# Half-block sums and key-value products as 128x64 TensorE tiles, two steps on GpSimd, and a new order of work, in a four-layer attention kernel

## The chip, the cores and the metric

The kernel runs on one core of one Trainium2 chip. The metric is the device time of one execution in microseconds. Two runs of the kernel before gave 414.84 and 413.82, median 414.33.

A core has five engines with a queue each: PE (TensorE, matrix products), ACT (ScalarE), DVE (VectorE), POOL (GpSimd) and SP (here it only starts transfers). Each runs its own instructions strictly in order. Between engines the kernel waits on semaphores.

## What is computed

```python
x = A_x                                  # [1, 2048, 512], bf16
x = x + A(layernorm(x))                  # linear attention, 32 heads of 16
x = x + B(layernorm(x))                  # sliding-window softmax attention
x = x + A(layernorm(x))
x = x + B(layernorm(x))

# A: q, k, v = split(x @ wqkv);  phi(t) = where(t > 0, t + 1, exp(t)) + 1e-6
kv  = einsum("bhsd,bhse->bhde", phi(k), v);  z = einsum("bhsd->bhd", phi(k))
num = einsum("bhqd,bhde->bhqe", phi(q), kv); den = einsum("bhqd,bhd->bhq", phi(q), z) + 1e-6
A   = (num / den) @ wo

# B: W = 256, softmax over the keys with 0 <= query - key < W
p = softmax(where(mask, q @ k.T * 16 ** -0.5, -1e9))
B = (p @ v) @ wo
```

In A every row needs the sums `kv` and `z` over all 2048 rows, so no row of a layer A can finish before the last row of the layer before it. A layer B needs only the 256 rows before.

## The kernel before, in words

**Tiles and stages.** The 2048 rows are 16 row blocks of 128. Prefixes of the operations name the stage: `1.` is layer 1's pass over keys and values, `2.` is layer 1's queries and output and layer 2 (`2.b.` projections, `2.a.` attention), `2k.` is layer 3's keys and values, and `3.` is layer 3's queries and output and layer 4. Layers 2 and 3 overlap block by block: while some blocks are still in the attention of layer 2, others already make keys of layer 3.

**Layer A.** `a_kv` makes phi(k) (`pk`) and v with a column of ones (`vA`), and `kv_mm` adds their product into PSUM. One weight tile of 128 columns holds 8 heads, so the 128x136 product contains all pairs of these 8 heads, of which only the 8 diagonal blocks of 16x17 are wanted. It takes 4 matmuls a row block. In pass 1 all blocks add into one pair of PSUM banks; in pass `2k.` groups of 4, 4, 4, 2, 1 and 1 blocks do, and `acc` adds each group into `kvacc` on DVE, two instructions a group. `sums` multiplies by the block-diagonal mask `bm8` into `kvz`. `a_q` makes phi(q) with an exponential (ACT, L884), a minimum (DVE, L885), a relu (ACT, L887) and an addition (DVE, L888). `a_out` multiplies with `kvz` (L947), divides (L956 to L959) and goes through the output projection.

**Layer B.** `b_qkv` projects and lays keys out per head; values go by a small transfer from POOL's queue (`vbd`, L990). `b_attn` handles one row block. Its window is cut into pieces of 64 keys: four inner pieces that all 128 query rows see (`pF`) and two outer ones that only 64 query rows each see (`pH`; blocks 0 and 1 have one outer piece). Scores run as 32-row tiles of the array, four heads side by side (L1016 for `pH`, L1065 for `pF`); ACT takes exponentials (L1044, L1086); DVE multiplies by triangular masks (L1052 for `pH`, L1104 for `pF`); then PE multiplies the weights with the values: the inner sums (L1134) and the half-block sums (L1122; L1170 for the last block, in `b_end`). A half-block sum has only 64 query rows. Before, it is a full 128-column weight tile all the same: `pH` has 192 columns a head, the middle 64 are kept at zero (filled once by `fill_pH`, L705), and the slice of 128 columns is [rows 0 to 63, zeros] for one outer piece and [zeros, rows 64 to 127] for the other.

**Order.** Nothing is scheduled on the device. `ORDER` is a table of operation numbers, written out; each engine runs its operations in that order, `'` marks the second of two possible engines (for copies out of PSUM: ACT or DVE), and the numbers behind `:` are PSUM banks and buffers. `_Sched` derives the waits from what each operation reads and writes.

**Tile shapes on PE.** An operation has a mode: `f` for full 128x128 weight tiles, `r` for the 32-row tiles of the scores. Where a projection stands ahead of a change of mode, its last 512 columns are issued as 448 and 64 (`cut` in `proj_tok`).

Of the kernel before, what the change touches and what calls it, by code (L numbers as in the profile page):

```python
# [7 lines left out]
dt = mybir.dt  # L8
# [310 lines left out]
def _act_cost(n):  # L319
    return 0.055 + 0.000833 * n  # L320
# [23 lines left out]
617:4.3 618 619:0 448:2 405 851:0.2.0 415 852 853 416 631 592 632 417:3 625:7.2.5 406 633:0 626 878:4.0.1 622:6.3 623 648 879 880 649 467:3.10.3 468 627' 854  # L344
620 624' 634:4 428:4.0 429 873 469 418:3 650 593 449:2 471 882:0.6.2 883 884 450 482:3.11.1 483 855:1 860:0 861 856 430 431 470 857 621 432:1 451 484 903
651:1 858:1 935:4.6.0 486 862 863:2 859:0 864 885 419:2 420 421 635:3.4 936 874:0.4.3 485 872 433:0 652:0 636 937 607:2.0.0 875 876 608 909:0.6.4 637':1 904
910 911 865:1 62 609' 640:3.0 641 666 653:2.5 638 913:0.4.5 628 654 914 915 643:7.1.1 644 877 886:6 639 667 881 642' 668 629 610 611 655':2 669:2 912 891:3
887 970:0.4.1 645 646 888 702 703 889:3 890:2 938 866:2 892 893 971 972 67 656 894:0 895 657 905:0.6.0 906 867 434:5 435 868 907 944:0.3.3 436 658:2.1 1391
945 908 946 458:6.1 659 459 684 460 472 661:5.2.2 662 670:1 461 660 685 1392 462:3 686 704 917:0.3.1 1393 663' 921:2 922 923 463:2 896:3 918 919 948:0.6.2
924:2 647 916 920 671:5.0 949 950 672 473:3.3 925:1 474 705:3 926:2 1394:0 1395:0 927 487 475 687:1 673:0 1005:0.6.2 1006 476 477:0 928 676:5.2 677 929:0 930  # L350
1007 940:0.3.0 941 464:2 465 897:7 951 942 678' 979:0.5.4 980 688:3 706:2 478:1 931:0 1008 939 466 898 674 1401:4.1 1402 899 981 943 947 952:0.2.5 953
# [78 lines left out]
"""  # L430
PHIA = ("1.k","2.q","3.q")
HMD = ("2.a.", "3.a.")
BYPE = {("x1.", t) for t in range(4)} | {("a2.", 15), ("k2.", 15), ("o3.", 0), ("x3.", 0), ("a3.", 15)} | {("o2.",0),("x2.",0)}
VMOVE = {"POOL": 1.03}
KNEAR = {("3.b.", 0)}
LATE = 1


class _Kernel:
# [496 lines left out]
    def bmask(self, hf):  # L936
        return self.bm8.h[:].unsqueeze(1).unsqueeze(3).to_broadcast([P, 2, 8, 17])
# [443 lines left out]
```

## Time and profile before

| | |
|---|---|
| median of the two runs | 414.33 us (413.82 to 414.84) |
| the profiled execution | 414.87 us |
| span of the profile (first to last instruction) | 413.6 us |
| instructions | 18932 |
| TensorE clock granted | 1.00 |
| transfers from POOL's queue (`vbd`) | 128, 2.3 us to landing |
| transposing transfers on SP's queue (`oT`) | 60, 2.6 us to landing |

Busy times of the engines, the chain of waits and the groups of instructions are shown in the prediction, where they are used. "Busy" of PE includes the time in which a matmul runs out through the array, so it can read 97% where the matmuls themselves are issued less densely; the distance from one matmul's start to the next's is the better price. A group's "idle before" is the time that its engine stood still just ahead of it, and the name behind the arrow is what ended that.

### The profile page before, as it was taken

The page shows a single profiled execution, that of the slowest core. Times are in us where ns is not written, and L with a number is a line of the kernel's source. Part 1 is how long each engine was busy: PE and PEld are TensorE (multiplying, and loading weights), DVE is VectorE, ACT ScalarE, POOL GpSimd, SP SyncE. Part 2 cuts the span into 40 slices and gives each one's busy share as a digit, 9 for nine tenths or more (in the row PEclk, how much of TensorE's full clock was granted, in tenths as well). Part 3 has the DMA queues.
Part 4 walks back from the last instruction along what each step waited for, and adds up shares of the span by engine and source line. Part 5 has one row for each costly group of instructions (what it writes and reads, how often), then busy time and mean ns, then how long its engine had stood idle before and what let it go on. Part 6 is the DMA issues. An engine that isn't in the chain of part 4 may idle for free.

```text
span 413.6 us, 18932 instructions
## 1 busy us (share of the span) xinstructions
PE 399.4 (97%) x8394; PEld 284.3 (69%) x8394; DVE 370.5 (90%) x979; ACT 376.6 (91%) x485; POOL 104.8 (25%) x204
## 2 busy tenths in 40 slices
PE   7999999999999999999999999999999999999998
PEld 2654877776676767777686678676767776867765
DVE  6996799999999999999998999999999999887873
ACT  5998769999999999999999467899999999999996
POOL 2420025162053121411313000260533232311300
DMA  8539224526243235222122102331375453261433
GB/s 259 145 84 217 43 61 80 101 60 99 46 55 57 48 51 69 50 35 61 42 49 55 41 2 40 70 75 32 80 81 76 68 107 34 55 93 30 58 54 92
DMA packets 76808, 29.48 MB, mean 71 GB/s; under 512 B 66352, under 2 KB 74672, under 8 KB 76720
## 3 DMA queue, kind: packets, MB, share of 16 engines
q1 hardware_dynamic: 71424, 22.63, 29.7%
q0 software_dynamic: 4096, 4.46, 6.1%
q8 instruction: 68, 1.11, 1.2%
q10 hardware_dynamic: 1200, 1.11, 0.9%
q14 instruction: 20, 0.16, 0.2%
HBM read 6.29 MB, written 2.10 MB: 20 GB/s over the span
## 4 chain that ended last, share of the span: by engine, by line
PE 50%; ACT 34%; DVE 11%; DMA 3%; issue 1%; SPq 0%; DVEq 0%
ACT pF L1086 24%; PE ps L863 21%; PE ps L875 10%; ACT pH L1044 7%; PE ps L1134 6%; PE ps L1065 5%; PE ps L1122 3%; DVE o L959 2%; DMA w_Av<-in_A_wqkv_dram 2%; PE ps L1016 1%; DVE stats L819 1%; DMA oT<-o 1%; PE ps L921 1%; PE ps L947 1%; DVE pk L890 1%
## 5 line engine op out<-in xcount | busy, mean ns | idle before, releaser
L1086 ACT ACTIVATE pF<-ps 128x1024 bf16<-128x1024 f32 x240 | 229.6, 1083 | 4.4 <-PE ps L1065 2.6
L822 POOL TENSOR_TENSOR rstd<-mv,const 128x1 f32<-128x1 f32 x64 | 37.6, 594 | 211.9 <-DVE mv L820 194.2
L990 POOL DMA_DIRECT2D vbd<-vt x128 | 67.3, 533 | 73.8 <-DVE vt L850 48.6
L1134 PE MATMUL ps<-vbd,pF 128*128 128x34 bf16 x1856 | 62.2, 178 | 1.9 <-issue 1.9
L1044 ACT ACTIVATE pH<-ps 128x1024 bf16<-128x1024 f32 (+1 forms) x64 | 60.3, 1014 | 2.6 <-PE ps L1016 2.3
L1134 PEld LDWEIGHTS ps<-vbd,pF 128*128 128x128 bf16 x1856 | 54.7, 96 | 8.4 <-issue 2.1
L1104 DVE TENSOR_TENSOR pF<-pF,const 128x512 bf16<-128x512 bf16 (+2 forms) x116 | 47.1, 413 | 5.6 <-ACT pF L1086 5.2
L1065 PE MATMUL ps<-qT,kbd 32*128 32x128 bf16 x1920 | 48.7, 217 | 1.9 <-ACT pF L1086 0.6
L884 ACT ACTIVATE E<-ps 128x512 bf16<-128x512 f32 x64 | 38.6, 622 | 10.4 <-PE ps L875 7.8
L819 DVE BATCH_NORM_STATS2 stats<-xres 128x6 f32<-128x512 bf16 x64 | 43.4, 684 | 1.9 <-DMA xres<-in_A_x_dram 1.6
L1052 DVE TENSOR_TENSOR pH<-pH,const 128x1024 bf16<-128x1024 bf16 (+1 forms) x64 | 41.1, 644 | 0.4 <-ACT pH L1044 0.4
L1065 PEld LDWEIGHTS ps<-qT,kbd 32*128 32x128 bf16 x1920 | 28.2, 92 | 17.7 <-ACT pF L1086 7.0
L875 PE MATMUL ps<-xT,w_Bk 128*128 128x128 bf16 x512 | 35.5, 219 | 0.7 <-ACT xT L850 0.3
L875 PE MATMUL ps<-xT,w_Bq 128*128 128x128 bf16 x512 | 35.6, 219 | 0.2 <-ACT pF L1086 0.2
L1122 PEld LDWEIGHTS ps<-vbd,pH 128*128 128x128 bf16 x928 | 29.2, 96 | 9.4 <-issue 3.1
L863 PE MATMUL ps<-w_Av,xTa 128*128 128x512 bf16 (+2 forms) x134 | 33.9, 369 | 1.4 <-DMA w_Av<-in_A_wqkv_dram 1.2
L875 PE MATMUL ps<-xTa,w_Aq 128*128 128x128 bf16 x512 | 34.8, 219 | 0.2 <-DVE pq L888 0.2
L863 PE MATMUL ps<-w_Bv,xT 128*128 128x512 bf16 (+2 forms) x144 | 34.2, 356 | 0.6 <-ACT pF L1086 0.3
L863 PE MATMUL ps<-w_Bo,oT 128*128 128x512 bf16 (+2 forms) x141 | 34.5, 354 | 0.3
L1122 PE MATMUL ps<-vbd,pH 128*128 128x34 bf16 x928 | 32.8, 178 | 1.3 <-DVE pF L1104 0.5
L863 PE MATMUL ps<-w_Ao,oT 128*128 128x512 bf16 (+2 forms) x145 | 33.7, 354 | 0.2
L863 PE MATMUL ps<-w_Ak,xTa 128*128 128x512 bf16 (+1 forms) x131 | 32.7, 374 | 0.6 <-ACT xTa L850 0.5
(98 smaller groups left out, 611.1 us busy)
## 6 DMA issues: line engine op xcount, KB each, us to landing
vbd<-vt POOLq DMA_DIRECT2D x128, 34.0 KB, 2.3
xres<-in_A_x_dram SPq DMA_DIRECT2D x16, 128.0 KB, 5.7
out_dram<-xres SPq DMA_DIRECT2D x15, 128.0 KB, 2.3
oT<-o SPq DMA_TRANSPOSE x60, 2.6
w_Ak<-in_A_wqkv_dram ACTq DMA_DIRECT2D x1, 512.0 KB, 5.5
w_Av<-in_A_wqkv_dram ACTq DMA_DIRECT2D x1, 512.0 KB, 7.6
w_Aq<-in_A_wqkv_dram SPq DMA_DIRECT2D x1, 512.0 KB, 6.6
w_Ao<-in_A_wo_dram SPq DMA_DIRECT2D x1, 512.0 KB, 5.8
```

The source lines that it names most:

```text
L819: s.op(n + ".st", {"DVE": 0.595}, lambda e, en: e.bn_stats(st0, x.h[:]), reads=[x], writes=[st])
L863: i = e.matmul(g.h[:, a:b], xT.h[:, kt, :], w.h[:, kt, a:b], start=(kt == 0), stop=(kt == 3), skip_group_check=True)
L875: i = e.matmul(g.h[:, f * P:(f + 1) * P], w.h[:, kt, f * P:(f + 1) * P], xT.h[:, kt, :], start=(f == 0 and kt == 0), stop=(kt == 3), skip_ ...
L884: s.op(n + ".e", {"ACT": _act_cost(512)}, lambda e, en: e.activation(E.h[:], g.h, ACT.Exp, bias=0.0), reads=[g], writes=[E])
L990: return [e.dma_start(vbd.h[64 * a:64 * a + 64, j, a], vt.h[64 * j:64 * j + 64, a]) for j in range(2)]
L1044: return e.activation(d, c, ACT.Exp, bias=0.0, scale=DH ** -0.5)
L1052: return e.tensor_tensor(v, v, tr, ALU.mult)
L1065: i = e.matmul(ss[r // 2].h[:, r % 2, k * P:k * P + P], kbds[fj[m] // 2].h[32 * r:32 * r + 32, f, fj[m] % 2, :], qT.h[32 * r:32 * r + 32, ...
L1086: s.op("e%d%d" % (u, g), {"ACT": _act_cost(1024)}, lambda e, en, S=ss[g], pb=pb, g=g: e.activation(pb.h[:, 2 * g:2 * g + 2, :], S.h, ACT.E ...
L1104: return e.tensor_tensor(v, v, tr, ALU.mult)
L1122: i = e.matmul(U.h[:, c:c + 34], pH.h[:, 4 * r + f, 64 * a:64 * a + P], vbds[j // 2].h[:, j % 2, :, 4 * f + r, :], start=first[0], stop=Tr ...
L1134: i = e.matmul(U.h[:, c:c + 34], pFs[at[f, m][0]].h[:, r, at[f, m][1] * P:at[f, m][1] * P + P], vbds[fj[m] // 2].h[:, fj[m] % 2, :, 4 * f ...
```

## The change

1. **Half-block sums as 128x64 tiles.** `pH` shrinks to 128 columns a head, without the zeros. The two outer pieces of a head become two matmuls with 64 weight columns each, at column positions 0 and 64 of the array (`tile_position=(0, 64 * a)`), writing PSUM partitions 0 to 63 and 64 to 127. This is a third mode, `c`. With two outer pieces the half sums open the accumulator, ahead of the inner ones; with one, they come behind. They no longer list the `pF` tiles among what they wait for.
2. **Key-value products as 128x64 tiles.** 8 matmuls of 64 weight columns and 68 moving columns a row block in place of 4 of 128 and 136. The result fits one PSUM bank; pass 1 issues them in four groups of four blocks; `acc` becomes one DVE instruction a group, and `sums` four DVE instructions of 136 columns in place of two of 272.
3. **Row block 15's queries in layer 3**: the exponential is taken on POOL as a power of e (`q.w`, `ALU.pow`); DVE makes min(q, 0) into `xm` and max(q, 0), and the closing addition also adds 1e-6. ACT's exponential and relu of that block go.
4. **Row block 9 in layer 4**: the two `pH` masks go from DVE to POOL.
5. A new `ORDER`; row block 3's first transposition goes from PE to a transfer; `fill_pH` goes.

```diff
-BYPE = {("x1.", t) for t in range(4)} | {("a2.", 15), ("k2.", 15), ("o3.", 0), ("x3.", 0), ("a3.", 15)} | {("o2.",0),("x2.",0)}
+BYPE = {("x1.", t) for t in range(3)} | {("a2.", 15), ("k2.", 15), ("o3.", 0), ("x3.", 0), ("a3.", 15)} | {("o2.",0),("x2.",0)}
-LATE = 1
+KV1 = [4, 4, 4, 4]
+KV2 = [4, 4, 4, 2, 1, 1]
+PHIP = set()
+POWQ = {("3.", 15)}
+MPOOL = {("3.a.", 9)}
...
-            self.r_pH = self.preset("pH", 3, [P, 16, 192], self.fill_pH())
+            self.r_pH = self.ring("pH", 3, [P, 16, P])
...
     def phi(self, n, g, E, o, view, t=None):
+        if n == "q" and (s.at[0], t) in POWQ:
+            xm, base = self.r_xm.buf(), self.base
+            s.op(n + ".n", {"DVE": _dve_cost(512)}, lambda e, en: e.tensor_scalar(xm.h[:], g.h, 0.0, None, op0=ALU.min), reads=[g], writes=[xm], new=[xm])
+            s.op(n + ".r", {"DVE": _dve_cost(512)}, lambda e, en: e.tensor_scalar(view(o), g.h, 0.0, None, op0=ALU.max), reads=[g], writes=[o])
+            s.op(n + ".w", {"POOL": 3.0}, lambda e, en: e.tensor_tensor(E.h[:], base.h[:].to_broadcast([P, D]), xm.h[:], ALU.pow), reads=[xm, base], writes=[E])
+            s.op(n + ".a", {"DVE": 0.335}, lambda e, en: e.scalar_tensor_tensor(view(o), E.h[:], 1e-6, view(o), op0=ALU.add, op1=ALU.add), reads=[E], writes=[o])
+            return
...
                 for f in range(4):
-                    i = e.matmul(d[f // 2][:, (f % 2) * 136:(f % 2) * 136 + 136], pk.h[:, f * P:(f + 1) * P],
-                                 vA.h[:, 8 * f:8 * f + 8, :], start=(start and n == 0 and f % 2 == 0), stop=True,
-                                 skip_group_check=True)
+                    for c in range(2):
+                        i = e.matmul(g.h[64 * c:64 * c + 64, f * 68:f * 68 + 68], pk.h[:, f * P + 64 * c:f * P + 64 * c + 64],
+                                     vA.h[:, 8 * f + 4 * c:8 * f + 4 * c + 4, :], start=(start and n == 0 and f == 0), stop=True,
+                                     skip_group_check=True, tile_position=(0, 64 * c))
...
-            s.op("mH%d" % g, {"DVE": 0.065 + 0.00054 * 512 * len(pcs)}, mkH, reads=[self.tri, mH[g]], part=[pH])
+            s.op("mH%d" % g, {"POOL": 1.5} if (s.at[0], t) in MPOOL else {"DVE": 0.065 + 0.00054 * 512 * len(pcs)}, mkH, reads=[self.tri, mH[g]], part=[pH])
...
                         for a, j in pcs:
                             c = ((f % 2) * 4 + r) * 34
-                            i = e.matmul(U.h[:, c:c + 34], pH.h[:, 4 * r + f, 64 * a:64 * a + P], vbds[j // 2].h[:, j % 2, :, 4 * f + r, :],
-                                         start=first[0], stop=True, skip_group_check=True)
-                            first[0] = False
+                            i = e.matmul(U.h[64 * a:64 * a + 64, c:c + 34], pH.h[:, 4 * r + f, 64 * a:64 * a + 64], vbds[j // 2].h[:, j % 2, :, 4 * f + r, :],
+                                         start=(len(pcs) == 2 and f == 2 * g and r == 0), stop=True, skip_group_check=True, tile_position=(0, 64 * a))
...
-            s.op("u%dh" % g, {"PE": 0.0255 * 8 * len(pcs)}, pvH, reads=[pH] + [vbds[j // 2] for _, j in pcs] + (pFs[2 * g:2 * g + 1 + LATE] if m0 == 0 else use(2 * g)),
-                 writes=[U], new=[U], kind="sum")
+                s.op("u%dh" % g, {"PE": 0.27 if side else 0.25}, pvH, reads=[pH] + [vbds[j // 2] for _, j in pcs], writes=[U], new=new, mode="c", kind="sum")
...
-                    for hf in range(2):
-                        d = self.kvacc[:, 2 * hf:2 * hf + 2, :].rearrange("p f c -> p (f c)")
-                        i = e.tensor_copy(d, g2[hf].h[:, 0:272]) if ngrp == 0 else e.tensor_tensor(d, g2[hf].h[:, 0:272], d, ALU.add)
-                    return i
+                    d = self.kvacc[:].rearrange("p f c -> p (f c)")
+                    return e.tensor_copy(d, g2.h[:, 0:272]) if ngrp == 0 else e.tensor_tensor(d, g2.h[:, 0:272], d, ALU.add)
```

How the order moves is shown at three places. The first is PE in the stretch where layer 2's attention and layer 3's keys and values interleave. Rows name line, operation, output and inputs, and the tile; `pH` rows are half-block sums, `pF` rows with `vbd` inner sums, `qT,kbd` scores. Before:

```order
L1065 MATMUL ps<-qT,kbd 128x128 x16
L1122 MATMUL ps<-vbd,pH 128x34 x16
L1134 MATMUL ps<-vbd,pF 128x34 x16
L1122 MATMUL ps<-vbd,pH 128x34 x16
L1134 MATMUL ps<-vbd,pF 128x34 x16
L1016 MATMUL ps<-qT,kbd 128x64 x32
L1134 MATMUL ps<-vbd,pF 128x34 x16
L875 MATMUL ps<-xT,w_Bq 128x128 x8
```

The same stretch after the change (lines have moved: L1064 is the inner scores, L1119 the half-block sums, L1135 the inner sums):

```order
L1064 MATMUL ps<-qT,kbd 128x128 x16
L860 MATMUL ps<-w_Bo,oT 128x512 x3
L860 MATMUL ps<-w_Bo,oT 128x448
L860 MATMUL ps<-w_Bo,oT 128x64
L1119 MATMUL ps<-vbd,pH 64x34 x16
L1064 MATMUL ps<-qT,kbd 128x128 x16
L1135 MATMUL ps<-vbd,pF 128x34 x16
L1119 MATMUL ps<-vbd,pH 64x34 x16
L1135 MATMUL ps<-vbd,pF 128x34 x16
L1016 MATMUL ps<-qT,kbd 128x64 x32
```

Before, half sums and inner sums follow each other in one tile shape; after, each group of half sums stands between others as a shape of its own (64x34). Counted along PE's whole order, the tile shape changes 306 times before and 380 times after, the projections cut into 448 and 64 columns are 59 and 82, and the matmuls of the half sums are 960 both times.

The second place is PE at the end of pass `2k.`, where the last key-value products of layer 3 are made and its queries' products (`kvz,pq`) begin. Before:

```order
L921 MATMUL ps<-vA,pk 128x136 x16
L863 MATMUL ps<-w_Ak,xTa 128x512 x4
L863 MATMUL ps<-w_Av,xTa 128x512 x4
L921 MATMUL ps<-vA,pk 128x136 x8
L863 MATMUL ps<-w_Av,xTa 128x512 x4
L921 MATMUL ps<-vA,pk 128x136 x4
L875 MATMUL ps<-xTa,w_Aq 128x128 x8
L921 MATMUL ps<-vA,pk 128x136 x4
L875 MATMUL ps<-xTa,w_Aq 128x128 x32
L947 MATMUL ps<-kvz,pq 128x136 x8
```

The same place after:

```order
L860 MATMUL ps<-w_Ak,xTa 128x512 x4
L860 MATMUL ps<-w_Av,xTa 128x512 x7
L860 MATMUL ps<-w_Av,xTa 128x448
L860 MATMUL ps<-w_Av,xTa 128x64
L925 MATMUL ps<-vA,pk 64x68 x64
L872 MATMUL ps<-xTa,w_Aq 128x128 x32
L947 MATMUL ps<-kvz,pq 128x136 x10
```

Before, the products of the last eight blocks stand in four groups with projections between them; after, they are one run of 64, with 32 matmuls of the query projection (`w_Aq`) between them and the first product with `kvz`. On DVE the four `kvacc` additions and the four `kvz` instructions that lie between these two stand directly behind each other.

The third place is DVE and POOL at the power of row block 15 in layer 3. DVE after the change, with buffer numbers; `xm` is the input of the power, `rstd` comes from POOL:

```order
L883 TENSOR_SCALAR xm_95<-ps 128x512
L902 TENSOR_TENSOR xres_23<-ps,xres_23 128x512 [waits s_PE]
L816 BN_STATS stats_1<-xres_23 128x6 [waits s_DVE]
L956 TENSOR_SCALAR dn_119<-ps 128x32 [waits s_PE]
L817 BN_AGGR mv_38<-stats_1 128x2 [waits s_DVE]
L958 RECIPROCAL dn_119<-dn_119 128x32 [waits s_DVE]
L959 TENSOR_TENSOR o_113<-ps,dn_119 128x512 [waits s_DVE]
L822 TENSOR_SCALAR xn_43<-xres_23,mv_38,rstd_39 128x512 [waits s_POOL]
```

And POOL:

```order
L819 TENSOR_TENSOR rstd<-mv,const 128x1
L885 TENSOR_TENSOR E<-const,xm 128x512
L819 TENSOR_TENSOR rstd<-mv,const 128x1
L990 DMA vbd<-vt 64x272 x4
```

On POOL the power stands ahead of the `rstd` that the last DVE row waits for. The result of the power itself is read 144 DVE rows after `xm` is written. Counted along ACT's order, copies out of PSUM on ACT change from 8 to 10 (`kt`), 12 to 9 (`qT`), 11 to 8 (`vt`) and 5 to 4 (`xTa`), and one small `oT` copy comes from DVE; on DVE they change from 23 to 21, 20 to 23 and 21 to 24.

More of the change, by code (lines that the diff above doesn't have):

```diff
@@ L1134, in pvF @@
                             i = e.matmul(U.h[:, c:c + 34], pFs[at[f, m][0]].h[:, r, at[f, m][1] * P:at[f, m][1] * P + P], vbds[fj[m] // 2].h[:, fj[m] % 2, :, 4 * f + r, :],
-                                         start=False, stop=True, skip_group_check=True)
+                                         start=(not side and f == 2 * g and r == 0 and m == m0), stop=True, skip_group_check=True)
                     return i
-                s.op("u%d%d" % (g, f % 2), {"PE": 0.0252 * 4 * (4 - m0)}, pvF, reads=use(f) + [vbds[j // 2] for j in fj[m0:]], writes=[U], kind="sum")
+                s.op("u%d%d" % (g, f % 2), {"PE": 0.0252 * 4 * (4 - m0)}, pvF, reads=use(f) + [vbds[j // 2] for j in fj[m0:]], writes=[U],
+                     new=[U] if not side and f == 2 * g else [], kind="sum")
+            if not side:
+                half([])
             dn = self.r_dn.buf()
@@ L1169, in pvH @@
                     for a, j in pcs:
-                        i = e.matmul(U.h[:, r * 34:r * 34 + 34], pH.h[:, 4 * r + f, 64 * a:64 * a + P], vbds[j // 2].h[:, j % 2, :, 4 * f + r, :],
-                                     start=(r == 0 and j == pcs[0][1]), stop=True, skip_group_check=True)
+                        i = e.matmul(U.h[64 * a:64 * a + 64, r * 34:r * 34 + 34], pH.h[:, 4 * r + f, 64 * a:64 * a + 64], vbds[j // 2].h[:, j % 2, :, 4 * f + r, :],
+                                     start=(r == 0), stop=True, skip_group_check=True, tile_position=(0, 64 * a))
                 return i
-            s.op("z%dh" % f, {"PE": 0.0255 * 4 * len(pcs)}, pvH, reads=[pH] + [vbds[j // 2] for _, j in pcs], writes=[U], new=[U], kind="sum")
+            s.op("z%dh" % f, {"PE": 0.145}, pvH, reads=[pH] + [vbds[j // 2] for _, j in pcs], writes=[U], new=[U], mode="c", kind="sum")
             for hf in range(2):
@@ L1306, in graph @@
         s.at = ("1.", base)
-        self.sums(lambda hf: kvS.h[:, hf, 0:272], kvz)
+        self.sums(lambda: kvS.h[:, 0:272], kvz)
         b1 = base + 0.1
@@ L1336, in graph @@
         s.at = ("2.", b2)
[L1337 removed]
+        self.sums(lambda: self.kvacc[:].rearrange("p f c -> p (f c)"), kvz2)
         self.segment("3.", b2, xTs2, kvz2, True)
```

217 lines of the change are left out of this document (110 added, 107 removed), and 70 rows, old and new, of the table ORDER.

## The prediction, made before the changed kernel had run

> **What bounds the kernel now.** I read the page's head first (span, busy time of each engine, shares of the chain that ended last), then the busy times by stage, then PE's timeline in the attention.
>
> ```profile
> span 413.6 us, 18932 instructions
> PE 399.4 (97%) x8394; PEld 284.3 (69%) x8394; DVE 370.5 (90%) x979; ACT 376.6 (91%) x485; POOL 104.8 (25%) x204
> PE 50%; ACT 34%; DVE 11%; DMA 3%; issue 1%; SPq 0%; DVEq 0%
> ```
>
> Three engines are at 90% or above, and the chain alternates between PE (half of the span) and ACT (a third). So no single engine can be made faster alone for full pay. By stage (stretch in us; then its length; then busy us and instructions of PE, weight loads, DVE, ACT, POOL; clock; DMA share; GB/s):
>
> ```profile
> 0.00:20.00 20.00, 17.10 (x120) 9.26 (x121) 16.25 (x56) 14.88 (x23) 6.45 (x23) 1.00 0.67 201
> 80.00:200.00 120.00, 117.51 (x2722) 84.87 (x2720) 112.37 (x286) 116.39 (x141) 35.74 (x66) 1.00 0.36 60
> 200.00:280.00 80.00, 77.89 (x1464) 57.15 (x1461) 74.75 (x200) 67.15 (x96) 17.56 (x32) 1.00 0.25 47
> 280.00:400.00 120.00, 116.99 (x3024) 85.02 (x3028) 108.21 (x267) 118.68 (x133) 32.99 (x62) 1.00 0.41 62
> ```
>
> In the two long attention stretches (240 us) PE is busy 234.5 us and ACT 235.1 us: both are full. Between 200 and 280, where the keys of layer 3 are made, ACT has 12.9 us to spare and PE 2.1 us. The clock is 1.00 throughout, so it plays no part.
>
> **Prices on PE.** Starts and busy time of PE's instructions in the attention of layer 4; a matmul's price is the distance from its start to the next start:
>
> ```profile
> 296.82 0.60 PE L863 MATMUL ps<-w_Bo,oT 128*128 128x512 bf16 x3
> 297.35 0.40 PE L1065 MATMUL ps<-qT,kbd 32*128 32x128 bf16 x16
> 297.68 0.61 PE L863 MATMUL ps<-w_Bo,oT 128*128 128x512 bf16 x2
> 298.13 0.56 PE L1122 MATMUL ps<-vbd,pH 128*128 128x34 bf16 x16
> 298.54 0.96 PE L1134 MATMUL ps<-vbd,pF 128*128 128x34 bf16 x32
> 299.43 0.40 PE L1065 MATMUL ps<-qT,kbd 32*128 32x128 bf16 x16
> 299.81 0.57 PE L1122 MATMUL ps<-vbd,pH 128*128 128x34 bf16 x16
> 300.23 1.03 PE L863 MATMUL ps<-w_Ao,oT 128*128 128x512 bf16 x5
> 301.19 0.41 PE L1016 MATMUL ps<-qT,kbd 32*128 32x64 bf16 x32
> 301.53 0.97 PE L1134 MATMUL ps<-vbd,pF 128*128 128x34 bf16 x32
> ...
> 311.35 0.40 PE L947 MATMUL ps<-kvz,pq 128*128 128x136 bf16 x4
> 311.58 0.60 PE L863 MATMUL ps<-w_Bo,oT 128*128 128x512 bf16 x3
> ```
>
> There is next to no gap between them: PE is issue-bound here. Half sums: 298.54 − 298.13 = 0.41 us for 16, so 25.6 ns each. The 128x136 product: 0.23 us for 4, 58 ns. A full 512-column product: 298.13 − 297.68 for two, 0.225 us.
>
> A change of tile shape: 32 inner sums at 25.6 ns would take 0.82 us but 0.89 pass to the scores at 299.43, so 0.07 us go on the way in. 16 scores of 128 columns, four side by side, stream as many columns as one 512-column product, 0.225 us; 0.33 pass (297.35 to 297.68), so 0.105 go on the way out; the 32 scores of 64 columns give 0.34 − 0.225 = 0.115. I take 0.088 us a change, the mean of 0.07 and 0.105, and keep 0.07 and 0.115 as ends. The same rows give what tiles side by side cost: 32 scores of 64 columns are 8 sets of four in 0.225 us, 28 ns a set.
>
> **The change on PE.**
>
> ```profile
> L1122 PE MATMUL ps<-vbd,pH 128*128 128x34 bf16 x928 | 32.8, 178 | 1.3 <-DVE pF L1104 0.5 <-ACT kt L850 0.2 <-ACT qT L850 0.2
> L1170 PE MATMUL ps<-vbd,pH 128*128 128x34 bf16 x32 | 1.4, 179 | 0.0
> L921 PE MATMUL ps<-vA,pk 128*128 128x136 bf16 x128 | 10.0, 223 | 0.1
> ```
>
> Half sums: 928 + 32 = 960. Blocks 0 and 1 of both layers B have one outer piece, 64 matmuls without a partner, whose price I leave. The other 896 become 448 pairs. Before, a pair costs 2 × 25.6 = 51.2 ns. No row shows two column tiles side by side. Below lies 25.6 ns (a pair for the price of one), above 51.2 (one after the other); the nearest row is the set of four row tiles, 28 ns, and I take 30. Gain 448 × 21.2 = 9.5 us, ends 0 and 11.5.
>
> Key-value products: 128 × 58 ns = 7.4 us become 128 pairs of 68 columns. From the same row, a little more for the wider tile, 32 ns: 4.1 us. Gain 3.3, ends 0.9 (51.2 a pair) and 3.8 (28).
>
> Changes of shape: 380 instead of 306, 74 × 0.088 = 6.5 us lost, ends 5.2 and 8.5. Net on PE 9.5 + 3.3 − 6.5 = **6.3 us less**, ends 10.1 less and 7.6 more. The 23 further cut projections issue the same columns; row block 3's four transposes that leave PE are four matmuls. I take both at nothing.
>
> **ACT and DVE.**
>
> ```profile
> L884 ACT ACTIVATE E<-ps 128x512 bf16<-128x512 f32 x64 | 38.6, 622 | 10.4 <-PE ps L875 7.8 <-PE ps L863 2.4
> L887 ACT ACTIVATE pq<-ps 128x512 bf16<-128x512 f32 x32 | 19.9, 634 | 2.9 <-PE ps L875 2.8
> L850 ACT ACTIVATE kt<-ps 128x512 bf16<-128x512 f32 x8 | 4.9, 616 | 1.7 <-PE ps L875 1.6
> L850 DVE CAST kt<-ps 128x512 bf16<-128x512 f32 x23 | 15.7, 681 | 0.3 <-PE ps L875 0.2
> L1328 DVE TENSOR_TENSOR kvacc<-ps,kvacc 128x272 f32<-128x272 f32 x10 | 3.9, 433 | 0.0
> L1232 DVE TENSOR_TENSOR kvz<-kvacc,const 128x272 bf16<-128x272 f32 x2 | 0.8, 438 | 0.0
> L1052 DVE TENSOR_TENSOR pH<-pH,const 128x1024 bf16<-128x1024 bf16 x56 | 37.8, 678 | 0.4 <-ACT pH L1044 0.4
> ```
>
> ACT loses block 15's exponential (0.62) and relu (0.63) and five copies net (+2 − 3 − 3 − 1, at 0.62: 3.1), and gains a small one I put at 0.3: **4.1 us less**. The filling of `pH` also goes, at the start, where ACT is busy only 14.9 of 20 us; I take it at nothing, since ACT waits there for the first projections.
>
> DVE gains four copies net (4 × 0.68 = 2.7) and loses six `kvacc` instructions (6 × 0.43 = 2.6). Four `kvz` instructions become eight of half the width: from the same time to twice 1.75 us, so 0 to 1.75 more. Block 15: two reads of 512 columns out of PSUM come (1.36), and one minimum goes. Two masks go (1.36). About 1 us more in 370, on an engine that has 11% of the chain: 0.1.
>
> At the end of pass `2k.` DVE makes four `kvacc` and four `kvz` instructions in a row, 4 × 0.43 + 4 × 0.22 to 0.44 = 2.6 to 3.5 us, while PE has 32 matmuls of the query projection in front of the first product that needs them. Before, two and two stood there (1.7 us) behind the same 32. PE will stand for what is not covered; with the products' own run of 32 pairs as further cover I put 0.5 us, ends 0 and 1.5.
>
> **POOL.**
>
> ```profile
> L822 POOL TENSOR_TENSOR rstd<-mv,const 128x1 f32<-128x1 f32 x64 | 37.6, 594 | 211.9 <-DVE mv L820 194.2 <-DVE dn L956 15.9 <-DVE const L724 1.7
> L731 POOL IOTA const<- 128x128 int32 x1 | 0.2, 227 | 0.0
> L735 POOL MEMSET const<- 128x1 f32 x1 | 0.1, 91 | 0.0
> L898 DVE TENSOR_TENSOR xres<-ps,xres 128x512 bf16<-128x512 f32 x32 | 21.7, 678 | 0.2 <-PE ps L863 0.2
> L819 DVE BATCH_NORM_STATS2 stats<-xres 128x6 f32<-128x512 bf16 x64 | 43.4, 684 | 1.9 <-DMA xres<-in_A_x_dram 1.6
> L958 DVE RECIPROCAL dn<-dn 128x32 f32<-128x32 f32 x32 | 10.9, 343 | 0.5
> L959 DVE TENSOR_TENSOR o<-ps,dn 128x512 bf16<-128x512 f32 x32 | 21.8, 684 | 0.5
> L1086 ACT ACTIVATE pF<-ps 128x1024 bf16<-128x1024 f32 x240 | 229.6, 1083 | 4.4 <-PE ps L1065 2.6 <-PE ps L1072 0.5
> ```
>
> The power over 512 columns has no row. `rstd` is the same operation on one column, 0.59 us, and an end from below; the index fill shows (227 − 91) / 127 = 1.1 ns a column for something much simpler, so 1.2 us is a better lower end, and 3 us my guess, from nothing better than between. Nobody needs its result soon (144 DVE instructions later). But the next `rstd` is queued behind it on POOL, and DVE waits for that one at `xn`. Between stand DVE's 0.68 + 0.68 + 0.34 + 0.68 = 2.4 us and two short ones; less the `rstd` itself, about 1.8 us cover the power. At 3 us DVE stands 1.2 us once, in a stretch where it is 93% busy. I count none of it in the time, since its later work is also fed late by PE, and keep 1.2 for the range; from there on every further us of the power is a us on DVE.
>
> The two masks (0.68 each on DVE) go ahead of four `vbd` transfers of a later block, and the first half sum of block 9 waits for POOL. In ACT's order six inner exponentials follow these two before the next half exponentials: four of them, some 4 us, lie ahead of the inner sum that PE issues right behind that half sum, so two masks of up to 2 us each are covered. None counted.
>
> The Trainium skill, page "SBUF — State Buffer", in the part on engine ports, says that DVE instructions with two SBUF inputs and GpSimd share one pair of ports as an exclusive lock for the whole instruction. By that rule these three POOL instructions would also hold up masks on DVE, and my sum would be up to their length, a few us, worse; no row here shows POOL with a long instruction.
>
> **The sum.** PE's part of the chain is 50% of 413.6, 207 us; PE's work shrinks by 6.3 of 399.4, which gives 3.3 us. ACT's part is 34%, 141 us; its work shrinks by 4.1 of 376.6, 1.5 us. Less 0.5 at pass `2k.` and 0.1 for DVE: 4.2 us. The profiled execution took 414.87 (span 413.6 and 1.3 around it), so 410.7; the median of the runs is 0.54 lower, so **410 us**, 1% faster. A measurement of this kernel tells about 2% (8.3 us) from no change, so this counts as "within 2%". With PE's and the stall's ends the forecast's own range is 405 to 414.
>
> **The rivals.**
>
> *The two column tiles don't run side by side.* Then the change doesn't do what it says: a pair still costs 51.2 ns, key-value products give 0.9 us, and 74 changes of shape cost 6.5: PE gets 5.6 us more work where it is issue-bound, and the time is **420 us, slower**. It decides from a pair price of some 41 ns on, where 448 × 10.2 + 128 × 17 ns = 6.7 us only just pays for the changes of shape; at 56 ns a pair it is slower by over 2%. For it: no row shows column tiles. Against: four row tiles in 28 ns show that the array takes several small tiles at once. The page "TensorEngine Tiling (Array Packing)" of the Trainium skill, in its restrictions, says that column tiling switches the fast weight load off, and "TensorE: Matmul & The Clock Gate", in its part on the weight load, gives the columns divided by 1.2 as the ns of a plain load: 53 ns for 64 columns, an estimate by which a pair would gain nothing even with both loads at once. No run here shows it yet. Chance 0.14.
>
> *PE's gain turns into waiting for ACT.* In 240 of 413 us ACT is as full as PE; if the shorter PE work only lets PE wait for exponentials there and ACT's 4.1 us come from stretches where it had time to spare, the time stays at **414**. For it: ACT is at 98% in those stretches. Against: ACT's copies that go lie there too. Chance 0.17.
>
> *All of it pays.* Pair at 26 to 28 ns, PE 10 us less, and the order moves exponentials into the 12.9 spare us between 200 and 280: **404**. Chance 0.12.
>
> *The power is long.* At 10 us on POOL, 8 us of waiting at `xn`, half of it recovered: **414 to 418**. Chance 0.06.
>
> **How the numbers follow.** Forecast 0.51. Faster by over 2% (under 406): most of the third rival (0.10) and the lower edge of the forecast (0.07), 0.17. Slower by over 2% (over 422.6): half of the first rival and a little of the last, 0.08. Within: 0.75. The range 404 to 419 leaves out 0.08 below and 0.11 above.
>
> **What would show it.** In the profile after, right: 16 half sums start to start in about 0.24 us plus a change; a change into or out of the narrow shape at 0.07 to 0.12; PE's rows still without gaps; ACT's busy time near 372. Wrong: half sums of 16 in 0.41 or more; `xn` on DVE waiting for `rstd` by more than a microsecond; PE standing behind exponentials by more in total than now; a gap in front of the first product with `kvz`.

## The result, and the profile after

| | before | after |
|---|---|---|
| median of two runs | 414.33 us | 487.73 us (487.33 to 488.12) |
| profiled execution | 414.87 us | 488.12 us |
| span of the profile | 413.6 us | 486.6 us |
| mean TensorE clock granted | 1.00 | 0.92 |

The ratio is 1.175 [1.169, 1.182]: 73 us slower than before. The prediction had said 410 us.

The page's head, the clock over 40 slices, and the shares of the chain, of the kernel after:

```profile
span 486.6 us, 19202 instructions
PE 400.4 (82%) x8541; PEld 278.7 (57%) x8541; DVE 374.7 (77%) x979; ACT 371.6 (76%) x478; POOL 193.7 (40%) x208
PEclk9999999999999999999999997555559999799999
ACT 35%; PE 28%; POOL 17%; DVE 15%; DMA 2%; issue 1%; SPq 0%; DVEq 0%; POOLq 0%
```

DVE and ACT are busy about as long as before; only POOL has 89 us more, and POOL, which had no share of the chain before, now has 17% of it, 83 us. So most of the loss lies in one place. The clock's dips at slices 25 to 30 and at slice 35 show where PE stood: a long stand and a short one.

The groups of instructions of the kernel after that answer to this (busy us, mean ns of one | idle of the engine just before them, and what ended it):

```profile
L885 POOL TENSOR_TENSOR E<-const,xm 128x512 bf16<-128x512 f32 x1 | 81.9, 81933 | 0.0
L819 POOL TENSOR_TENSOR rstd<-mv,const 128x1 f32<-128x1 f32 x64 | 39.5, 621 | 182.0 <-DVE mv L817 173.6
L822 DVE TENSOR_SCALAR xn<-xres,mv,rstd 128x512 bf16<-128x512 bf16 x64 | 25.2, 398 | 70.5 <-POOL rstd L819 70.4
L947 PE MATMUL ps<-kvz,pq 128*128 128x136 bf16 x128 | 14.0, 226 | 69.2 <-DVE o L959 68.6
```

The power over 512 columns takes 81.9 us. `rstd` is one number a row for the layer norm, made on POOL, and `xn` the rows that DVE normalizes with it. The wait at `xn` for `rstd` is in the table with 70.4 us, and PE's wait behind it with 68.6.

The long stand in order of time, on POOL, then DVE, then PE (start, length, engine, line, operation; in brackets the engine's idle time before it and what ended that):

```profile
276.77 0.56 POOL L819 TENSOR_TENSOR rstd<-mv,const 128x1 f32<-128x1 f32 x1 [2.52 <-DVE mv L817]
277.31 81.93 POOL L885 TENSOR_TENSOR E<-const,xm 128x512 bf16<-128x512 f32 x1
359.22 0.54 POOL L819 TENSOR_TENSOR rstd<-mv,const 128x1 f32<-128x1 f32 x1
...
288.39 0.41 DVE L1103 TENSOR_TENSOR pF<-pF,const 128x512 bf16<-128x512 bf16 x1
...
290.80 0.42 DVE L1150 SCALAR_TENSOR_TENSOR o<-dn,ps 128x256 bf16<-128x256 f32 x1
359.80 0.41 DVE L822 TENSOR_SCALAR xn<-xres,mv,rstd 128x512 bf16<-128x512 bf16 x1 [68.58 <-POOL rstd L819]
...
361.99 0.63 PE L947 MATMUL ps<-kvz,pq 128*128 128x136 bf16 x4 [68.58 <-DVE o L959]
362.42 1.06 PE L860 MATMUL ps<-w_Bo,oT 128*128 128x512 bf16 x2
363.27 1.91 PE L860 MATMUL ps<-w_Bv,xT 128*128 128x512 bf16 x4
364.98 0.76 PE L860 MATMUL ps<-w_Bo,oT 128*128 128x512 bf16 x3
365.67 0.40 PE L1064 MATMUL ps<-qT,kbd 32*128 32x128 bf16 x16
```

POOL goes straight from one `rstd` into the power, and the next `rstd` runs when the power ends. DVE is at the `xn` that needs it from 291.2 on and stands 68.6 us; everything else is queued behind that `xn` on DVE, and PE stops 2 us later. When PE starts again, its 512-column products lie 0.43 us apart (362.42 to 364.98 for six) where they otherwise lie 0.22 apart: with the rows beside them some 1.6 us more. The clock granted in this profile is 1.00 until 297.0, some 3.6 us after PE's last matmul (293.4), and 0.50 from there to 365.3. The Trainium skill, page "TensorE: Matmul & The Clock Gate", in the section "What's actually happening", says that an idle window of some 3.4 us brings the array to half its clock; these 3.6 us agree.

The short stand, at row block 9's masks in layer 4, POOL, DVE and PE:

```profile
411.10 4.80 POOL L1051 TENSOR_TENSOR pH<-pH,const 128x1024 bf16<-128x1024 bf16 x2 [1.78 <-ACT pH L1043]
...
410.97 0.68 DVE L1051 TENSOR_TENSOR pH<-pH,const 128x1024 bf16<-128x1024 bf16 x1
411.57 4.61 DVE L1103 TENSOR_TENSOR pF<-pF,const 128x512 bf16<-128x512 bf16 x2
416.10 0.25 DVE L1148 RECIPROCAL dn<-ps 128x16 f32<-128x16 f32 x1
...
412.95 0.40 PE L1064 MATMUL ps<-qT,kbd 32*128 32x128 bf16 x16
416.95 0.62 PE L1119 MATMUL ps<-vbd,pH 128*64 128x34 bf16 x16 [3.60 <-DVE o L1150]
417.50 1.10 PE L1135 MATMUL ps<-vbd,pF 128*128 128x34 bf16 x32
...
419.90 1.91 PE L860 MATMUL ps<-w_Bv,xT 128*128 128x512 bf16 x5
421.75 0.61 PE L1064 MATMUL ps<-qT,kbd 32*128 32x128 bf16 x16
```

Two masks on POOL take 4.80 us, 2.4 each. Beside them two of DVE's masks, 0.41 us each elsewhere, take 4.61 together, and PE stands 3.60. Here too PE comes back at a lower rate: 16 narrow half sums take 0.55 us (416.95 to 417.50) where a line below shows 0.37, and the five products of `w_Bv` take 1.85 (419.90 to 421.75), against 0.96 in the kernel with the masks back on DVE. The granted clock is 0.50 from 416.5 to 423.3.

### The profile page after: what moved, and what is told of

Its sections match the earlier page's. It is cut to its first block, busy times and chain, and to the rows that moved or that the text cites. A ratio compares the mean times of both kernels' runs of the same rounds, so it can differ in the third digit from the quotient of the medians.

```text
span 486.6 us, 19202 instructions
## 1 busy us (share of the span) xinstructions
PE 400.4 (82%) x8541; PEld 278.7 (57%) x8541; DVE 374.7 (77%) x979; ACT 371.6 (76%) x478; POOL 193.7 (40%) x208
## 4 chain that ended last, share of the span: by engine, by line
ACT 35%; PE 28%; POOL 17%; DVE 15%; DMA 2%; issue 1%; SPq 0%; DVEq 0%; POOLq 0%
ACT pF L1085 25%; POOL E L885 17%; PE ps L860 11%; PE ps L872 6%; ACT pH L1043 6%; PE ps L1135 4%; PE ps L1064 3%; ACT E L888 2%; DVE o L959 2%; DVE pF L1103 2%; ACT pq L891 1%; DVE stats L816 1%; DMA w_Aq<-in_A_wqkv_dram 1%; PE ps L1119 1%; PE ps L1016 1%
## 5 line engine op out<-in xcount | busy, mean ns | idle before, releaser
L819 POOL TENSOR_TENSOR rstd<-mv,const 128x1 f32<-128x1 f32 x64 | 39.5, 621 | 182.0 <-DVE mv L817 173.6
L885 POOL TENSOR_TENSOR E<-const,xm 128x512 bf16<-128x512 f32 x1 | 81.9, 81933 | 0.0
L822 DVE TENSOR_SCALAR xn<-xres,mv,rstd 128x512 bf16<-128x512 bf16 x64 | 25.2, 398 | 70.5 <-POOL rstd L819 70.4
L947 PE MATMUL ps<-kvz,pq 128*128 128x136 bf16 x128 | 14.0, 226 | 69.2 <-DVE o L959 68.6
L1135 PE MATMUL ps<-vbd,pF 128*128 128x34 bf16 x1856 | 60.8, 179 | 0.0
L1135 PEld LDWEIGHTS ps<-vbd,pF 128*128 128x128 bf16 x1856 | 54.3, 96 | 7.2
L847 ACT ACTIVATE vt<-ps 128x512 bf16<-128x512 f32 x8 | 5.0, 624 | 69.8 <-PE ps L860 69.8
L1064 PE MATMUL ps<-qT,kbd 32*128 32x128 bf16 x1920 | 49.5, 218 | 3.2 <-issue 0.6
L1103 DVE TENSOR_TENSOR pF<-pF,const 128x512 bf16<-128x512 bf16 (+2 forms) x116 | 49.9, 446 | 2.4 <-ACT pF L1085 2.1
L947 PEld LDWEIGHTS ps<-kvz,pq 128*128 128x128 bf16 x128 | 8.8, 99 | 73.4 <-DVE o L959 68.8
L1064 PEld LDWEIGHTS ps<-qT,kbd 32*128 32x128 bf16 x1920 | 28.9, 93 | 20.0 <-ACT pF L1085 7.5
L1051 DVE TENSOR_TENSOR pH<-pH,const 128x1024 bf16<-128x1024 bf16 (+1 forms) x62 | 39.4, 641 | 0.7 <-ACT pH L1043 0.7
L860 PE MATMUL ps<-w_Bv,xT 128*128 128x512 bf16 (+2 forms) x146 | 36.5, 368 | 0.1
```

What stands on the lines that cost most here:

```text
L819: s.op(n + ".rs", {"POOL": 0.53}, lambda e, en: e.tensor_tensor(a_rs, v, self.half.h[:], ALU.pow), reads=[mv, self.half], writes=[rs])
L860: i = e.matmul(g.h[:, a:b], xT.h[:, kt, :], w.h[:, kt, a:b], start=(kt == 0), stop=(kt == 3), skip_group_check=True)
L885: s.op(n + ".w", {"POOL": 3.0}, lambda e, en: e.tensor_tensor(E.h[:], base.h[:].to_broadcast([P, D]), xm.h[:], ALU.pow), reads=[xm, base], ...
L1064: i = e.matmul(ss[r // 2].h[:, r % 2, k * P:k * P + P], kbds[fj[m] // 2].h[32 * r:32 * r + 32, f, fj[m] % 2, :], qT.h[32 * r:32 * r + 32, ...
L1103: return e.tensor_tensor(v, v, tr, ALU.mult)
L1135: i = e.matmul(U.h[:, c:c + 34], pFs[at[f, m][0]].h[:, r, at[f, m][1] * P:at[f, m][1] * P + P], vbds[fj[m] // 2].h[:, fj[m] % 2, :, 4 * f ...
```

## The experiments

The first four ran on one chip, where the kernel before took 414.13 us (median of 29 runs), the next four on a second (414.21, median of 20), the last on a third; each ratio is to the kernel before on the same chip.

**The power goes back to ACT.** The kernel after, with layer 3's block 15 as all other blocks; in `ORDER` ACT's exponential and relu stand where DVE's two steps stood, and DVE's minimum where the power stood.

```diff
-POWQ = {("3.", 15)}
+POWQ = set()
```

> The changed kernel with row block 15's exponential, minimum and relu back on ACT and DVE; all else, the two masks on POOL and the order among them, stays. Theory (the power's 81.9 us stand in POOL's queue ahead of an rstd, so DVE waits 68.6 us at xn and everything behind it): 68.6 us go, and the 1 to 2 us that PE lost at half its clock after standing still: 416 to 419 us. Rival (the narrow tiles or the new order hold the kernel up in other places, and DVE would have waited there anyway): over 425 us.

Measured 415.95 us, ratio 1.0045 [1.0022, 1.0068], at the low end of what was expected. Taking out the one step gives back 72 of the 73 us. What is left still has the short stand, in the same three lengths (timeline of this kernel):

```profile
339.35 4.80 POOL L1051 TENSOR_TENSOR pH<-pH,const 128x1024 bf16<-128x1024 bf16 x2 [1.79 <-ACT pH L1043]
339.83 4.61 DVE L1103 TENSOR_TENSOR pF<-pF,const 128x512 bf16<-128x512 bf16 x2
345.21 0.61 PE L1119 MATMUL ps<-vbd,pH 128*64 128x34 bf16 x16 [3.60 <-DVE o L1150]
```

**The masks go back to DVE as well.**

```diff
-POWQ = {("3.", 15)}
-MPOOL = {("3.a.", 9)}
+POWQ = set()
+MPOOL = set()
```

> As the one before, and the two half-block masks of row block 9 back on DVE, at the places in the order where POOL had them. Theory (two masks of 2.4 us each on POOL hold up two masks on DVE for as long, so PE stands still for 3.6 us and runs at half its clock for some 2.5 us after that): 5 to 6 us less than with the masks on POOL, 411 to 413 us, so narrow tiles and new order are a small gain. Rival (the masks were covered, and the narrow tiles with 74 more changes of tile shape cost more than they save): 415 to 418 us, slower than the kernel before.

Measured 411.73 us, ratio 0.9944 [0.9923, 0.9965]: 0.6% faster than before, a gain that is left to the narrow tiles, ACT's relief and the new order together. Against the run above, the two masks on POOL cost 4.2 us, where 5 to 6 were expected. Head of the page, chain, two of the stretches that the prediction showed, and a few of PE's rows of this kernel:

```profile
PE 386.1 (94%) x8461; PEld 276.7 (67%) x8541; DVE 370.6 (90%) x980; ACT 372.0 (91%) x480; POOL 106.4 (26%) x205
ACT 51%; PE 34%; DVE 9%; DMA 3%; issue 2%; SPq 1%; POOL 0%; DVEq 0%; POOLq 0%
...
80.00:200.00 120.00, 113.94 (x2737) 82.81 (x2764) 115.18 (x290) 116.85 (x140) 34.94 (x65) 1.00 0.32 58
280.00:400.00 120.00, 112.51 (x3051) 83.41 (x3071) 108.12 (x267) 117.92 (x131) 32.77 (x62) 1.00 0.38 67
...
240.10 1.34 PE L925 MATMUL ps<-vA,pk 128*64 128x68 bf16 x64
241.38 1.96 PE L872 MATMUL ps<-xTa,w_Aq 128*128 128x128 bf16 x32
243.66 0.83 PE L947 MATMUL ps<-kvz,pq 128*128 128x136 bf16 x10 [0.32 <-DVE kvz L1238]
...
309.76 0.43 PE L1119 MATMUL ps<-vbd,pH 128*64 128x34 bf16 x16
310.13 0.40 PE L1064 MATMUL ps<-qT,kbd 32*128 32x128 bf16 x16
```

Sixteen narrow half sums with one change of shape take 0.37 us; less a change of 0.07 to 0.115 that is 0.255 to 0.30, or 32 to 38 ns a pair. Thirty-two pairs of key-value products with a change take 1.28 us (240.10 to 241.38); less 0.09, 37 ns a pair. In the two attention stretches PE is now busy 226.5 of 240 us (234.5 before) and ACT still 234.8 (235.1): PE has got room, ACT has not, and ACT's part of the chain is 51% (34% before).

**The half sums alone, in the order of before.** The kernel before, with the half sums of blocks with two outer pieces as pairs of narrow tiles; 432 pairs, and 383 changes of tile shape where before has 306.

```diff
+                            if len(pcs) == 2:
+                                i = e.matmul(U.h[64 * a:64 * a + 64, c:c + 34], pH.h[:, 4 * r + f, 128 * a:128 * a + 64], vbds[j // 2].h[:, j % 2, :, 4 * f + r, :],
+                                             start=(f == 2 * g and r == 0), stop=True, skip_group_check=True, tile_position=(0, 64 * a))
+                                continue
...
-                 writes=[U], new=[U], kind="sum")
+                 writes=[U], new=[U], mode=("c" if len(pcs) == 2 else "f"), kind="sum")
```

> The kernel before, in its own order, with the half-block sums of row blocks 2 to 15 of layer 2 and 2 to 14 of layer 4 as pairs of 128x64 tiles, nothing else. 432 pairs, 383 changes of tile shape in place of 306. Theory (a pair costs about 33 ns in place of 51, a change 0.09 us): PE gets 432 x 18 = 7.8 us less and 77 x 0.09 = 6.9 more, so the time stays within 1 us of before, 413 to 415 us. Rival (narrow weight tiles load slowly, or a change into them costs more than one into the scores): 418 us or more. A second rival (pairs overlap fully at 26 ns): 410 us.

Measured 413.70 us, ratio 0.9992 [0.9973, 1.0012]: no difference. At 35 ns a pair, 432 × (51.2 − 35) = 7.0 us are gained and 77 × 0.088 = 6.8 lost in changes of shape. By these prices the narrow half sums pay only in an order that needs fewer changes of shape for them.

**The power alone, in the order of before.** The kernel before with `phi`'s new branch and nothing else (with `xm` in bf16; `POWQ` as after).

> The kernel before with row block 15's exponential as a power on POOL and nothing else; its input tile is bf16 in place of float32, for space. Theory (the power's own length stalls the kernel, whatever the order and the tiles): a power of 80 us, DVE waiting 60 to 75 us for an rstd, 475 to 490 us. Rival (the power is long only because of its float32 input, or because POOL shares something with the narrow tiles): a power under 10 us and a time under 420 us.

Measured 492.06 us in one run. Rows of this kernel, a group and two waits (us in total, times, longest us):

```profile
L890 POOL TENSOR_TENSOR E<-const,xm 128x512 bf16<-128x512 f32 x1 | 82.2, 82202 | 0.0
DVE xn L827 <- POOL rstd L824: 72.7, 5, 70.8
...
PE ps L1131 <- DMA vbd<-vt: 72.3, 1, 72.3
```

It is 78 us over before, a little above what was expected. The power alone makes a loss of that size in the old order too, with the same wait at `xn`, 70.8 us at its longest. Here the wait at `xn` is not the only one: a `vbd` transfer is queued on POOL behind the power as well, and PE stands 72.3 us for it. So everything that POOL's queue holds behind a long instruction is late, not only an `rstd`.

**The power over 64 columns.** The kernel after, in its own order; 448 of the 512 columns of that block's exponential are left out.

```diff
-lambda e, en: e.tensor_tensor(E.h[:], base.h[:].to_broadcast([P, D]), xm.h[:], ALU.pow)
+lambda e, en: e.tensor_tensor(E.h[:, 0:64], base.h[:].to_broadcast([P, 64]), xm.h[:, 0:64], ALU.pow)
```

> The changed kernel with the power taken over the first 64 of its 512 columns only; the other 448 columns of row block 15's exponential are left as they lie in the tile. Theory (a fixed price a column, about 160 ns, and a cover of 13.3 us: in the changed kernel the power began at 277.3 us and DVE came to the waiting xn at 291.2, less 0.6 for the rstd): 64 columns take 10.6 us and are covered, DVE waits under 1 us at that xn, and the time is that with the power on ACT or a little less, 414 to 417 us. Rival (it is not the length: the power starts late, or its place ahead of the rstd alone costs): DVE still waits for several us, over 420 us.

Measured 416.56 us, ratio 1.0065 [1.0044, 1.0086], as without any power (1.0045). POOL and DVE at the power in this kernel:

```profile
275.99 10.53 POOL L885 TENSOR_TENSOR E<-const,xm 128x64 bf16<-128x64 f32 x1
286.50 0.54 POOL L819 TENSOR_TENSOR rstd<-mv,const 128x1 f32<-128x1 f32 x1
...
289.47 0.42 DVE L1150 SCALAR_TENSOR_TENSOR o<-dn,ps 128x256 bf16<-128x256 f32 x1
289.81 0.48 DVE L822 TENSOR_SCALAR xn<-xres,mv,rstd 128x512 bf16<-128x512 bf16 x1
```

A power of 10.5 us is covered whole: `rstd` is done at 287.04, and DVE comes to `xn` at 289.8. So in this order it is not a power on POOL as such that costs, but its length beyond some 13 us.

**Full-width half sums in the new order.** The kernel with power and masks back, with all half sums as 128-column tiles again and `pH` with its zeros; 316 changes of shape.

> The kernel with power and masks back on ACT and DVE, in the new order, with all half-block sums as full 128-column tiles again (zeros beside the 64 rows, filled once at the start); key-value products stay narrow. 316 changes of tile shape in place of 380. Theory (448 pairs at 34 ns against 51, and 64 changes at 0.09 us): PE gets 7.7 us more and 5.8 us less, so it is about 1 to 2 us slower than with narrow half sums, 412 to 414 us. Rival (narrow half sums are what made that kernel faster than before, by 2.4 us or more): 414 us or more. Second rival (they cost more than they bring): under 411 us.

Measured 412.95 us, ratio 0.9968 [0.9954, 0.9981]. So some of the gain is there without narrow half sums: with the narrow key-value products, ACT's relief and the new order. Which of these three brings it no run separates. The next run shows what the narrow half sums add.

**The kernel with power and masks back, beside it.**

> The kernel with power and masks back on ACT and DVE once more, for comparison with full-width half sums on the same chip. Both theories: as before, 0.994 of the kernel before, 411 to 412.5 us.

Measured 412.16 us, ratio 0.9948 [0.9927, 0.9968]. The narrow half sums are worth some 0.8 us in the new order; the two intervals overlap, so that this size is not settled. By the prices above it would be 448 × 16.2 = 7.3 us gained and 64 × 0.088 = 5.6 lost on PE.

**Prices on POOL.** A kernel with powers and products of several widths on POOL, and a stream of small operations on DVE beside the first of them.

> A small program of its own that computes nothing of the reference: POOL runs a power of e over 1, 16, 64 and 128 float32 columns and over 64 bf16 columns, a power of 64 columns to -0.5 as rstd is, and products of 1024, 512 and 64 bf16 columns, one after the other, while DVE runs products of two 512-column bf16 tiles and of one tile by a constant in turn. Theory: the power costs a fixed part of 0.4 us and 160 ns a column, of either type and either form, so 0.6, 3.0, 10.6, 21, 10.6 and 10.6 us; DVE's products of two tiles run at 0.4 us beside all powers and stop for the whole length of each long POOL product (2.4 us for 1024 columns). Rival (the length of the power depends on what is beside it on DVE, or DVE waits for powers too): durations that don't grow with the columns, and DVE standing for most of the powers' time.

Groups of POOL in this kernel:

```profile
L41 POOL TENSOR_TENSOR pw<-base,xf 128x64 bf16<-128x64 f32 x1 | 65.9, 65902 | 0.0
L41 POOL TENSOR_TENSOR pw<-base,xf 128x128 bf16<-128x128 f32 x1 | 20.7, 20720 | 0.0
L41 POOL TENSOR_TENSOR pw64b<-base,x 128x64 bf16<-128x64 f32 x1 | 10.5, 10510 | 0.0
L51 POOL TENSOR_TENSOR ml<-x,y 128x1024 bf16<-128x1024 bf16 x1 | 2.1, 2108 | 0.0
```

From 64 to 128 columns (20.72 − 10.51) / 64 = 160 ns a column; 512 columns at that price are 82 us. The first row is odd: this power began 8.1 us into the profile and ended 10.4 us after DVE's unbroken stream did, as if it could not begin while that ran; powers of 1 and 16 columns just ahead of it were not held. Why is open. The products ran when DVE had ended, so this kernel says nothing on the masks.

**Who holds whom.**

> A small kernel that computes nothing of the reference. Six phases: GpSimd makes two products of 128x1024 bf16 tiles in SBUF (three phases), or one power over 64 columns (three phases), and VectorE, let go just after GpSimd, makes ten operations: products of two 128x512 bf16 tiles in SBUF, operations on one such tile and a number, or copies of a 128x512 fp32 tile out of PSUM. In the changed kernel a VectorE product that takes 0.41 us alone lay 4.61 us beside two GpSimd masks of 2.4 us, and beside the power of 82 us VectorE's products kept their 0.41 us. Theory: the GpSimd product holds VectorE's two-tile products for its length (one or two of the ten take 2 us or more, the others 0.41), and the power holds nothing (all thirty operations beside it at their own 0.3 to 0.7 us). Rival: VectorE was held for another reason there, and all sixty run at their own length. Second rival: the hold goes the other way, as in the kernel of GpSimd's prices: GpSimd waits until VectorE's ten are done, so that its products seem to take 4 us and more and VectorE's are as ever.

Groups of this kernel, DVE's ten operations beside POOL's two products (`_by_ml`) and beside its power (`_by_pw`):

```profile
L36 DVE TENSOR_TENSOR two_by_ml<-x,y 128x512 bf16<-128x512 bf16 x10 | 7.2, 788 | 0.5 <-POOL t_ml_two L45 0.5
L37 DVE TENSOR_SCALAR one_by_ml<-x 128x512 bf16<-128x512 bf16 x10 | 5.9, 664 | 0.3 <-POOL t_ml_one L45 0.3
L38 DVE CAST psm_by_ml<-pt 128x512 bf16<-128x512 f32 x10 | 6.1, 681 | 0.3 <-POOL t_ml_psm L45 0.3
...
L36 DVE TENSOR_TENSOR two_by_pw<-x,y 128x512 bf16<-128x512 bf16 x10 | 3.5, 420 | 0.3 <-POOL t_pw_two L45 0.3
L37 DVE TENSOR_SCALAR one_by_pw<-x 128x512 bf16<-128x512 bf16 x10 | 2.2, 288 | 0.3 <-POOL t_pw_one L45 0.3
L38 DVE CAST psm_by_pw<-pt 128x512 bf16<-128x512 f32 x10 | 6.1, 681 | 0.3 <-POOL t_pw_psm L45 0.3
```

Beside POOL's products, DVE's products take 7.2 us in place of 3.5 and its one-tile operations 5.9 in place of 2.2, 3.7 more each time; copies out of PSUM take 6.1 both times. Beside the power nothing is held. The theory stands for the masks, and is too narrow in one point: DVE's operation on a single SBUF tile is held as well. Each product on POOL, 2.1 to 2.2 us long here, holds one DVE operation for about its own length: the first DVE row lasts 2.24 us.

```profile
5.03 2.24 DVE L36 TENSOR_TENSOR two_by_ml<-x,y 128x512 bf16<-128x512 bf16 x1 [0.46 <-POOL t_ml_two L45]
```

## Why the prediction was wrong, step by step

**The step that failed is POOL's power**, "3 us my guess, from nothing better than between", with "I count none of it in the time" and 1.2 us kept for the range. It takes 81.9 us. Both rows under that guess were one-column or much simpler work: `rstd` is 0.59 us for one column and the index fill 1.1 ns a column. The price is 160 ns a column, 145 times the lower end. The prediction did see that one row, `rstd`, was the same operation, and took it as an end from below only; the upper end, that every column costs what the first does, 512 × 0.59 = 302 us, was never written down. No row set a length between 1.2 and 302 us, so a chance of 0.06 for a power that is long was far too small.

**The same step had the wrong `xn`.** The prediction computed 1.8 us of cover, because a `xn` stands seven rows behind `xm` on DVE, and took its `rstd` for the one behind the power; the part on the change says the same of the order. All `rstd` share one name and one tile, so the order's rows could not tell them apart, and the reading was wrong: that `xn` ran at 256.4 us, five more `rstd` ran between `xm` and the power, and the `xn` that waits comes later. From `xm` at 253.2 to the stand, DVE did some 95 operations (window of the kernel after: length, then PE, weight loads, DVE, ACT, POOL):

```profile
253.20:291.30 38.10, 36.58 (x794) 26.84 (x792) 36.30 (x95) 34.95 (x46) 23.12 (x18) 1.00 0.34 59
```

The power started at 277.3 and DVE came to the `xn` at 291.2, so 13.9 us, less 0.6 for `rstd`, were covered: 13.3 us. The arithmetic closes: 81.9 − 13.3 = 68.6, the stand. And the run with a 10.5 us power shows that cover at work.

**The rival "The power is long"** had the mechanism and the place, with 10 us as its price. At 10 us it would have cost nothing, as the run with 10.5 us shows. Its "half of it recovered" was wrong for a length of this kind: every engine stood, and nothing was left to catch up with.

**The two masks**, "up to 2 us each are covered. None counted", are the second failure: 2.4 us each, and 4.2 us of time. Not the wait for their result did it, which the cover was counted for, but DVE's hold: two of DVE's own masks, of the block before, took 4.6 us beside them, and PE waited 3.6 us for DVE's normalization behind those (`[3.60 <-DVE o L1150]` at L1119 in the timeline above; the half sums that waited are block 8's, which need no mask from POOL). With the power on ACT and these masks on POOL, PE needs 10.6 us from the scores ahead of the stand to the scores behind its products (341.21 to 351.84); with the masks on DVE the same rows take 5.6 (341.58 to 347.17). Of these 5.0 us, 3.5 are the stand and 1.5 half clock. They are more than the 4.2 that the run without them won: there the two masks take 1.29 us on DVE, and PE waits 1.0 us for DVE a little later (348.57). The prediction quoted the Trainium skill, page "SBUF — State Buffer", on the lock on the ports that DVE and GpSimd share, with "a few us, worse" for three instructions. For the masks the rule was right and the sum should have carried it. That page of the Trainium skill, in its section "Who interferes with whom", also counts copies and one-tile operations in DVE's two-port modes among those that can be held, and leaves out an operation outside these modes with at most one SBUF input. The one-tile operations' 5.9 against 2.2 us agree, and so do the 6.1 against 6.1 us of the copies out of PSUM, which have no SBUF input. For the power the rule did not hold: in the 14 us that DVE worked beside it, its masks kept their 0.41 us (288.39 in the timeline above).

**The terms on PE** had the right mechanism and too large a size. A pair was put at 30 ns (measured 32 to 38), the key-value pair at 32 (37), a change of shape at 0.088 us; the measured pair prices are worked out with changes of 0.07 to 0.115 us, so no run measures the two apart. With these, 448 × 16.2 + 128 × 21 ns − 6.5 = 3.4 us on PE in place of 6.3. **ACT's** busy time fell by 5.0 us (376.6 to 371.6) where 4.1 were counted, and by 4.6 with block 15's steps back on ACT. Of both, 1.5 us are the filling of `pH` at the start (L705, one instruction of 1.5 us), which the prediction had set aside; so 3.5 and 3.1 are left. **The stall at the end of pass `2k.`**, put at 0.5 us, is 0.32. By the prediction's own method that is 207 × 3.4 / 399.4 = 1.8 us for PE and 141 × 3.1 / 376.6 = 1.2 for ACT, less 0.4: some 2.5 us; the kernel with power and masks back gains 2.4 and 2.1 on two chips. "PE's rows still without gaps" failed: PE has room now while ACT is as full as before, which the rival *PE's gain turns into waiting for ACT* had described, though the gain did not vanish as it said.

**"The two column tiles don't run side by side"** fell: 32 to 38 ns a pair, against its 51.2 and the 41 from which it decides. The Trainium skill, page "TensorEngine Tiling (Array Packing)", in its restrictions, says that column tiling switches the fast weight load off; whether it was off no run shows, but the loss that was worked out from it did not come.

**What the 73 us consist of:** −2.4 (narrow tiles, ACT's relief and the order; on the other chip −2.1), +4.2 (masks on POOL), +71.8 (power: 415.95 to 487.73), which is the measured 73.4 to within 0.2. Of the last, 68.6 are the stand and 1.6 the half clock after it; 1.6 are not pinned to a row.

## What to carry to other kernels

An operation that no row prices for its width needs both ends written down, the same operation's price per element times the number of elements among them; and when these lie far apart, what is queued behind it on its engine decides how much is at risk. Work that is moved to GpSimd is not free while GpSimd idles: two masks of 0.7 us on DVE took 2.4 us each on GpSimd and held DVE's own masks for that time. A narrower tile pays by the pair and costs by the change of shape, so count both before: by the prices above, the half sums gained 7 us here and lost 6 to 7.

## What was not expected of the hardware

- The power on GpSimd takes 160 ns a column of 128 partitions, in fp32 or bf16 input alike (10.53 and 10.51 us for 64), 82 us for 512 columns, where a product of two bf16 tiles takes 2.1 us for 1024.
- A GpSimd power of 82 us left DVE alone for the 14 us that DVE worked beside it, and a product of 2.1 us holds one DVE operation. The other way round, one power of 64 columns took 65.9 us beside DVE's unbroken stream and ended its own length after it; why that one and not the shorter ones is not settled.
- A stand of 3.6 us on PE was enough for half clock, and after the one at the masks PE worked at it for over 6 us (416.95 to 423.3), against 3.3 us after the long stand (361.99 to 365.3).
